# Gate and up products of one feed-forward block taken together, and a larger count for an exponential in the build-time planner

## The chip, the cores and the metric

The kernel runs on one core of a Trainium2 chip. The metric is the device time of one execution in microseconds (us); lower is better. The kernel before was timed three times: median 841.97 us, from 841.73 to 842.75.

## The reference

The input x (2048 rows of 512, bf16) goes through two branches, and a gate of one number per row mixes them:

```
g = sigmoid((x * gate_w).sum(-1, keepdims=True))
a = attention(x, wqkv) @ wo      # 32 heads of 16, no mask, softmax over 2048 keys
b = (silu(x @ w_gate) * (x @ w_up)) @ w_down     # 512 -> 1792 -> 512
return g * a + (1 - g) * b
```

Most of the work by far is the softmax: 32 heads x 2048 x 2048 exponentials. A head is only 16 wide, so the matmuls on either side of the exponential use a part of the array's rows or columns.

## The kernel before, in words

**Tiling.** Queries are cut into 4 blocks of 512 (QB), heads into 8 groups of 4 (G). One pair of these is a unit; there are 32. In a unit the keys are 16 tiles of 128 (KT). One key tile of one unit needs four score blocks, 128 keys by 512 queries, one for each head.

**Two ways to an exponential.** A score block goes one of two ways.
- ScalarE: two blocks at once into a two-bank PSUM tile (`s_t`, matmuls at most 64 rows high, two side by side), then one `Exp` over 128 x 1024 into `e_t` (`emit_pair`, L722). There are two such score tiles, so the score matmuls of pair k wait until the exponential of pair k-2 has read its tile.
- VectorE: one block into a single bank (`d_t`), one `tensor_scalar` from there into 16-bit integers (`y_t`), and after four of these, some passes over 128 x 2048 (`z_t`, `u_t`, two products) that correct the result. The last addition is made by a DMA that accumulates from GpSimd's queue (L802), or, for a tile near the end, by VectorE (`add_here`). `emit_d` (L755) holds this.

Either way the result is multiplied with the values in `o_ps` matmuls (four of 32 columns side by side, `pv`, L862), which collect in one bank per unit.

**The feed-forward branch and other side work.** It runs between the scores. For each query block there are 14 feed-forward blocks of 128 columns (FC). One has a gate product and an up product of four 128-row steps each. `two_banks` (L378) runs two accumulations at a time: each step is split into an upper and a lower half of 64 rows, and the halves of bank a and bank b run side by side. ScalarE takes tanh of the gate bank (`th`); VectorE makes `gs = (th + 1) * gate` from it and then `mt = 0.5 * gs * up`. `down_pieces` (L677) multiplies `mt` with w_down, 14 steps for two row tiles at once (`dps_a`, `dps_b`), and VectorE scales the result into `bblk`. `fin_pieces` and, for the last query block, `last_pieces` (L957, `a_l`) and `tail` (L963, `al`) apply wo and add.

Three single PSUM banks (`m_tile`, L335) serve all of this: gate and up, `dps`, `a_ps`, `a_l`, the q, k and v projections and every `d_t`. A two-bank piece starts only when two of them are free.

**What sets the order.** The Python code is a planner. At build time it keeps clocks for TensorE, VectorE and ScalarE (`plan.pe`, `plan.dve`, `plan.act`), adds a constant for each instruction it emits, and picks what comes next. Every instruction is then tied to its predecessor on its engine, so the order on the chip is the one that the planner wrote; the chip adds only waits. The numbers that matter here:
- `ACT_US` (L745): 0.906 counted for an exponential of 1024 columns. From it follow `s_end`, when a score tile is free, and `room`, how much time TensorE has before the next score pair; side work is put in as far as it fits.
- `v_unit` (L1290) gives a key tile to VectorE when its clock plus a lead is short of the time at which ScalarE would get there.
- A filler of four narrow matmuls (`o_ps<-xT`) is emitted where over 0.4 us of room are left and TensorE had little work just before.
- Side work is a list of chains with release and due slots (`Pacer`, L47). `pace.credit` grows with what is due. A chain waits for its predecessors.
- `later` queues a VectorE operation with its expected ready time and, optionally, a key; `fill_dve` avoids taking two with the same key one after the other, since `spend_v` adds 0.13 for that.

**Gate and up before.** `gu_chain(i)` (L630) puts the gate product of block i and the up product of block i-1 into one two-bank run. There are 57 chains for 56 blocks: the first has only a gate product and the last only an up product, each in one bank and at full height. At the end of a chain the product `gated` of block i-1, whose `gs` is there from the chain before, drains the up bank; tanh and then `gs` of block i drain the gate bank. `w_load` fetches up weights one block and gate weights two blocks ahead.

**The end.** When only one `o_ps` group is left, `tail(0)` completes all chains still open in the order of their due slots, and issues the first five of ten `al` matmuls. The last `o_ps` group follows, then the other five, the denominators of the last unit (`dt`, `rt`, `rps`), its scaled output, the last wo products, and four stores. This is the same in both kernels.

Of the kernel before, what the change touches and what calls it, by code (L numbers as in the profile page):

```python
# [9 lines left out]
ALU = mybir.AluOpType  # L10
AX = mybir.AxisListType
BF16 = mybir.dt.bfloat16
# [66 lines left out]
def kernel(  # L79
# [12 lines left out]
    nc = tc.nc  # L92
    P = 128
    x = A_x.flatten_outer_dims()
    S, D = x.shape
    F = B_w_gate.shape[1]
# [4 lines left out]
    DC = D // P  # L101
    FC = F // P
    KT = S // P
    QBW = 512
    QB = S // QBW
# [26 lines left out]
    work = ctx.enter_context(tc.tile_pool(name="work", bufs=2))  # L132
    etp = ctx.enter_context(tc.tile_pool(name="etp", bufs=EB))
    vex = ctx.enter_context(tc.tile_pool(name="vex", bufs=1))
    ffnw = ctx.enter_context(tc.tile_pool(name="ffnw", bufs=3))
# [20 lines left out]
    def mm(*args, **kw):  # L156
        return ordered(nc.tensor.matmul(*args, **kw))  # L157
# [10 lines left out]
    vec = Ordered()  # L168


    xT = big.tile([P, DC, S], BF16, name="xT")
# [4 lines left out]
    for c0 in (D, 0):  # L176

        nc.scalar.dma_start(out=wqk[:, :, c0:c0 + 64],
                            in_=A_wqkv[:, c0:c0 + 64].rearrange("(dc p) c -> p dc c", p=P))
# [29 lines left out]
    mt = big.tile([P, FC, QBW], BF16, name="mt")  # L209
# [39 lines left out]
    for h in range(8):  # L249
        c = 2 * (h % 4) + h // 4  # L250
# [32 lines left out]
    plan = Plan()  # L283
# [5 lines left out]
    def spend(mode, mms, ready=0.0):  # L289

        plan.seq += 1
        work_at.append((plan.pe, mms))
        plan.pe = max(plan.pe + (0.1 if mode != plan.mode else 0.0), ready) + (0.226 if mode == "F" else 0.216) * mms
        plan.mode = mode

    def later(cost, f, ready=None, key=None):

        c = plan.chain
        if c is not None:
            c.owed += 1  # L300
        ready = plan.pe + 0.25 if ready is None else ready
        owed.insert(sum(o[0] <= ready for o in owed), (ready, cost, f, c, key))
# [75 lines left out]
    def two_banks(n, name, a, b, end, stop=True):  # L378

        st = {}  # L380

        def pc(k):
            v, i = divmod(k, n)

            def f():
                if k == 0:
                    while m_ready(2) is None:
                        stuck()
                    st["a"], st["b"] = m_tile(name + "_a"), m_tile(name + "_b")
                if k == n:  # L390
                    sync(ordered(nc.tensor.nop()), st["half"])
                    spend("R", 0.1 if st["seq"] < plan.seq else 1.5)
                for ps, (w, r), h in ((st["a"], a(i), v), (st["b"], b(i), 1 - v)):
                    rows = slice(64 * h, 64 * h + 64)
                    st["half"] = mm(ps[:, :], lhsT=w[rows, :], rhs=r[rows, :], start=(k == i == 0),
                                    stop=(stop and k == 2 * n - 1), tile_position=(64 * h, 0), skip_group_check=True)
                spend("R", 1)
                st["seq"] = plan.seq
                if k == 2 * n - 1:
                    end(st["a"], st["b"])  # L400
            return f
        return [(1, pc(k), 2 if k == 0 else 0, "R", st if k == n else None) for k in range(2 * n)]
# [213 lines left out]
        later(0.5, end, plan.act + 0.2)  # L616


    FS = [(qb, fc) for qb in range(QB) for fc in range(FC)]
    w_gate, w_up, gs_of = {}, {}, {}  # L620

    def w_load(i, gate):
        if i < len(FS):
            w = ffnw.tile([P, DC, P], BF16, tag="wg" if gate else "wu", name="wg" if gate else "wu")
            fc = FS[i][1]
            nc.sync.dma_start(out=w[:], in_=(B_w_gate if gate else B_w_up)[:, fc * P:(fc + 1) * P].rearrange(
                "(dc p) f -> p dc f", p=P))
            (w_gate if gate else w_up)[i] = w

    def gu_chain(i):  # L630

        def rows(w_of, k):
            return lambda dc: (w_of[k][:, dc, :], xT[:, dc, FS[k][0] * QBW:(FS[k][0] + 1) * QBW])

        def gated(up):
            vec.scalar_tensor_tensor(out=mt[:, FS[i - 1][1], :], in0=gs_of.pop(i - 1)[:], scalar=0.5, in1=up[:, :],
                                     op0=ALU.mult, op1=ALU.mult)
            m_free(up, plan.dve)

        def gate(gp):  # L640
            th = work.tile([P, QBW], BF16, tag="th", name="th")
            flush_act(plan.pe + 0.4)
            act(out=th[:], in_=gp[:, :], func=ACT.Tanh, scale=0.5)
            plan.act = max(plan.act, plan.pe + 0.25) + 0.48

            def f():
                gs = work.tile([P, QBW], BF16, tag="gs", name="gs")
                vec.scalar_tensor_tensor(out=gs[:], in0=th[:], scalar=1.0, in1=gp[:, :], op0=ALU.add, op1=ALU.mult)
                m_free(gp, plan.dve)
                gs_of[i] = gs  # L650
            later(0.6, f, plan.act + 0.25)

        def both(gp, up):
            later(0.6, lambda: gated(up))
            gate(gp)

        if 0 < i < len(FS):
            return two_banks(DC, "gu", rows(w_gate, i), rows(w_up, i - 1), both)
        st = {}
        get, end = (rows(w_gate, 0), gate) if i == 0 else (rows(w_up, i - 1), lambda p: later(0.6, lambda: gated(p)))  # L660

        def pc(h):
            def f():
                if h == 0:
                    st["p"] = m_tile("gu")
                for dc in (2 * h, 2 * h + 1):
                    w, r = get(dc)
                    mm(st["p"][:, :], lhsT=w, rhs=r, start=(dc == 0), stop=(dc == DC - 1))
                spend("F", 2)
                if h == 1:  # L670
                    end(st["p"])
            return f
        return [(2, pc(0), True), (2, pc(1), False)]

    scaled = set()

# [65 lines left out]
        pairs[0] += 1  # L742

    exps = []
    ACT_US = 0.906  # L745

    def flush_act(before=None):

# [302 lines left out]
    for v in range(2):  # L1051
        vec.scalar_tensor_tensor(out=q0[0][:, v, :], in0=bp0[:, :], scalar=vsel[:, v:v + 1],
                                 in1=q0[0][:, v, :], op0=ALU.mult, op1=ALU.add)
# [3 lines left out]
                            op0=ALU.is_gt, op1=ALU.mult)  # L1057
    vec.scalar_tensor_tensor(out=bsel[:, :], in0=lo_t[:], scalar=0.5, in1=far_t[:],
                                   op0=ALU.is_lt, op1=ALU.mult)
# [47 lines left out]
    gates = [pace.add(gate_pieces(2 * i), 36 + 7 * i, 44 + 7 * i) for i in range(KT // 2)]  # L1107
    gates = [pace.add([(0.2, gate_end, False)], 40, 106, gates)]

    prev = []  # L1110
    fin_prev = []
    f0, f1 = 72, SLOTS - 8
    per = (f1 - f0) / QB
    for qb in range(QB):
        a0 = f0 + per * qb
        for i in range(FC * qb + (qb > 0), FC * qb + FC + 1):
            pcs = gu_chain(i)

            def first(f=pcs[0][1], i=i):
                if i == 0:  # L1120
                    w_load(0, True)
                    w_load(0, False)
                    w_load(1, True)
                w_load(i + 1, False)
                w_load(i + 2, True)
                f()
            pcs = [(pcs[0][0], first) + pcs[0][2:]] + pcs[1:]
            c = pace.add(pcs, 58, a0 + per * (0.6 if qb < QB - 1 else 0.68) * (i + 1 - FC * qb) / (FC + 1), prev)
            prev = [c]
        for tq in range(0, TQ, 2):  # L1130
            c = pace.add(down_pieces(qb, tq), 0 if qb else 100, a0 + per * (0.6 + 0.3 * (tq + 2) / TQ if qb < QB - 1 else 0.68 + 0.32 * (tq + 2) / TQ), prev + fin_prev + gates)
            prev = [c]
        last = qb == QB - 1
        fin_prev = []
        if last:
# [321 lines left out]
```

## Time and profile before

| what | before |
|---|---|
| median of 3 runs | 841.97 us |
| profiled execution, own time | 841.97 us |
| its span (first to last instruction) | 840.3 us |
| ScalarE busy | 815.2 us (97%) |
| VectorE busy | 785.5 us (93%) |
| TensorE matmuls busy | 759.7 us (90%) |
| mean granted TensorE clock | 0.998 |

The span is what the instructions of the program cover; 1.67 us of the execution's own time lie around it. A group in the profile is named by line, engine, operation and its tiles (output<-inputs); all matmuls have L157, all ScalarE instructions L160 and nearly all VectorE instructions L166, because helpers record them, so the tiles tell them apart. Busy time of TensorE is modelled for its end, and instructions overlap: an exponential of 1173 ns does not hold up the next for as long. Steps between starts are therefore taken from timelines.

### The profile page before, as it was taken

The page shows a single profiled execution, that of the slowest core. Times are in us where ns is not written, and L with a number is a line of the kernel's source. Part 1 is how long each engine was busy: PE and PEld are TensorE (multiplying, and loading weights), DVE is VectorE, ACT ScalarE, POOL GpSimd, SP SyncE. Part 2 cuts the span into 40 slices and gives each one's busy share as a digit, 9 for nine tenths or more (in the row PEclk, how much of TensorE's full clock was granted, in tenths as well). Part 3 has the DMA queues.
Part 4 walks back from the last instruction along what each step waited for, and adds up shares of the span by engine and source line. Part 5 has one row for each costly group of instructions (what it writes and reads, how often), then busy time and mean ns, then how long its engine had stood idle before and what let it go on. Part 6 is the DMA issues. An engine that isn't in the chain of part 4 may idle for free. (4 is left out here: it accounts for less than half of the span.)

```text
span 840.3 us, 16080 instructions
## 1 busy us (share of the span) xinstructions
PE 759.7 (90%) x5987; PEld 260.4 (31%) x6020; DVE 785.5 (93%) x1141; ACT 815.2 (97%) x916; POOL 94.9 (11%) x120
## 2 busy tenths in 40 slices
PE   7899899899989999999899998898999988998986
PEld 3222232233333333233333332222333322332322
DVE  6999998989999989999999899989999999999895
ACT  3999999999999999999999999999999999999996
POOL 5010100100101011110111101010011011000110
PEclk9999999999999999999999999999999999999999
DMA  9432252544455433554445435453544445363240
GB/s 204 128 70 45 57 98 58 108 92 86 96 104 111 92 80 73 108 114 92 99 88 107 80 87 105 92 107 74 104 90 80 91 95 108 89 124 60 58 95 26
DMA packets 101127, 77.18 MB, mean 92 GB/s; under 512 B 77728, under 2 KB 89592, under 8 KB 101048
## 3 DMA queue, kind: packets, MB, share of 16 engines
q0 software_dynamic: 12384, 45.09, 28.7%
q1 hardware_dynamic: 86792, 30.60, 15.5%
q8 instruction: 47, 0.77, 0.4%
q10 hardware_dynamic: 1872, 0.46, 0.2%
q14 instruction: 32, 0.26, 0.1%
HBM read 20.83 MB, written 2.34 MB: 28 GB/s over the span
## 5 line engine op out<-in xcount | busy, mean ns | idle before, releaser
L160 ACT ACTIVATE e_t<-s_t 128x1024 bf16<-128x1024 f32 x850 | 797.0, 1173 | 5.3 <-PE s_t L157 5.2
L157 PE MATMUL s_t<-qx,kaug 64*128 64x512 bf16 x1376 | 279.3, 380 | 51.0 <-ACT e_t L160 44.6
L157 PEld LDWEIGHTS <-kaug 64*128 64x128 bf16 x2048 | 140.3, 93 | 341.4 <-issue 306.5
L166 DVE TENSOR_SCALAR y_t<-d_t 128x512 uint16<-128x512 f32 x348 | 229.0, 682 | 17.9 <-PE d_t L157 15.1
L157 PE MATMUL o_ps<-e_t,vaug 128*32 128x512 bf16 x1700 | 160.0, 389 | 3.0 <-DVE osb L166 2.9
L157 PE MATMUL gu_b<-xT,wu 64*128 64x512 bf16 x440 | 133.1, 375 | 0.4 <-DVE y_t L166 0.2
L157 PE MATMUL gu_a<-xT,wg 64*128 64x512 bf16 x440 | 132.4, 375 | 0.0
L157 PE MATMUL d_t<-qx,kaug 64*128 64x512 bf16 x288 | 105.3, 377 | 4.6 <-DVE y_t L166 1.6
L157 PEld LDWEIGHTS <-vaug 128*32 128x32 bf16 (+1 forms) x2084 | 44.8, 94 | 139.0 <-issue 138.1
L802 POOL DMA_DIRECT2D y_t<-u_t x43 | 40.5, 943 | 356.2 <-PE s_t L157 165.6
L802 POOL DMA_DIRECT2D y_t<-kaug x36 | 36.6, 1016 | 294.8 <-PE s_t L157 141.3
L157 PE MATMUL dps_b<-wd_t,mt 64*128 64x512 bf16 x224 | 65.6, 375 | 0.0
L157 PE MATMUL dps_a<-wd_t,mt 64*128 64x512 bf16 x224 | 65.3, 375 | 0.0
L166 DVE TENSOR_SCALAR z_t<-y_t 128x2048 uint16<-128x2048 uint16 x87 | 60.1, 691 | 2.1
L166 DVE TENSOR_SCALAR y_t<-y_t 128x2048 uint16<-128x2048 uint16 x87 | 59.5, 684 | 1.4 <-DMA y_t<-kaug 1.4
L166 DVE TENSOR_TENSOR u_t<-u_t 128x2048 f16<-128x2048 f16 x43 | 52.6, 1223 | 1.1
L166 DVE TENSOR_TENSOR u_t<-u_t,z_t 128x2048 f16<-128x2048 f16 x43 | 52.3, 1216 | 0.0
L157 PE MATMUL s_t<-q,kaug 64*128 64x512 bf16 x216 | 43.8, 386 | 4.7 <-ACT e_t L160 4.0
L166 DVE TENSOR_TENSOR kaug<-kaug 128x2048 f16<-128x2048 f16 x37 | 45.2, 1222 | 0.9
L157 PEld LDWEIGHTS <-wg 64*128 64x128 bf16 (+1 forms) x444 | 41.2, 94 | 15.6 <-issue 1.8
L157 PEld LDWEIGHTS <-wu 64*128 64x128 bf16 (+1 forms) x444 | 41.3, 94 | 12.7 <-issue 0.9
L166 DVE TENSOR_TENSOR kaug<-kaug,z_t 128x2048 f16<-128x2048 f16 x37 | 45.0, 1215 | 0.0
(136 smaller groups left out, 631.0 us busy)
## 6 DMA issues: line engine op xcount, KB each, us to landing
y_t<-u_t POOLq DMA_DIRECT2D x43, 512.0 KB, 4.9
y_t<-kaug POOLq DMA_DIRECT2D x36, 512.0 KB, 4.9
wg<-in_B_w_gate_dram SPq DMA_DIRECT2D x56, 128.0 KB
wu<-in_B_w_up_dram SPq DMA_DIRECT2D x56, 128.0 KB
y_t<-wd_t POOLq DMA_DIRECT2D x7, 512.0 KB, 4.6
on<-osb SPq DMA_DIRECT2D x120, 16.0 KB
rb<-rr SPq DMA_DIRECT2D x15, 128.0 KB
wd_t<-in_B_w_down_dram SPq DMA_DIRECT2D x7, 256.0 KB
```

The source lines that it names most:

```text
L157: return ordered(nc.tensor.matmul(*args, **kw))
L160: ordered(nc.scalar.activation(*args, **kw))
L166: return lambda *a, **kw: ordered(f(*a, **kw))
L802: nc.gpsimd.dma_start(out=ya, in_=ua, accum_op=ALU.add)
```

## The change

Three edits:
1. `gu_chain(qb, fc)` now pairs the gate product and the up product of the same block. There are 56 chains, all of two banks. When one ends, tanh is emitted, and two VectorE operations, `gate` (makes `gs`, frees the gate bank) and `gated` (makes `mt`, frees the up bank), are queued with the same ready time, behind the tanh, and the same key.
2. Both weights of a block are loaded together, two blocks ahead. The due slots are spread over 14 chains a query block, not 15.
3. `ACT_US` is 0.92 in place of 0.906.

The loop in `tail` that completes open chains is not touched.

```diff
-    def gu_chain(i):
...
-        def gated(up):
-            vec.scalar_tensor_tensor(out=mt[:, FS[i - 1][1], :], in0=gs_of.pop(i - 1)[:], scalar=0.5, in1=up[:, :],
-                                     op0=ALU.mult, op1=ALU.mult)
-            m_free(up, plan.dve)
...
-        def both(gp, up):
-            later(0.6, lambda: gated(up))
-            gate(gp)
-
-        if 0 < i < len(FS):
-            return two_banks(DC, "gu", rows(w_gate, i), rows(w_up, i - 1), both)
...
+    def gu_chain(qb, fc):
+        st = {}
+
+        def load():
...
+        def done_gu(gp, up):
             th = work.tile([P, QBW], BF16, tag="th", name="th")
             flush_act(plan.pe + 0.4)
             act(out=th[:], in_=gp[:, :], func=ACT.Tanh, scale=0.5)
             plan.act = max(plan.act, plan.pe + 0.25) + 0.48
 
+            def gate():
+                st["gs"] = work.tile([P, QBW], BF16, tag="gs", name="gs")
+                vec.scalar_tensor_tensor(out=st["gs"][:], in0=th[:], scalar=1.0, in1=gp[:, :],
+                                         op0=ALU.add, op1=ALU.mult)
                 m_free(gp, plan.dve)
+
+            def gated():
+                vec.scalar_tensor_tensor(out=mt[:, fc, :], in0=st["gs"][:], scalar=0.5, in1=up[:, :],
+                                         op0=ALU.mult, op1=ALU.mult)
+                m_free(up, plan.dve)
+            later(0.6, gate, plan.act + 0.25, (qb, fc))
+            later(0.6, gated, plan.act + 0.25, (qb, fc))
+        return load, two_banks(DC, "gu", rows("g"), rows("u"), done_gu)
...
-    ACT_US = 0.906
+    ACT_US = 0.92
...
-                w_load(i + 1, False)
-                w_load(i + 2, True)
+                if ahead:
+                    gu[ahead][0]()
...
-            c = pace.add(pcs, 58, a0 + per * (0.6 if qb < QB - 1 else 0.68) * (i + 1 - FC * qb) / (FC + 1), prev)
+            c = pace.add(pcs, 58, a0 + per * (0.6 if qb < QB - 1 else 0.68) * (fc + 1) / FC, prev)
```

Since the planner works with clocks, these edits move instructions far from where they stand. Counted in the two built programs:

| instructions | before | changed |
|---|---|---|
| exponentials on ScalarE (`e_t`, 1024 columns) | 850 | 848 |
| key tiles on VectorE (`y_t`, four blocks each) | 87 | 88 |
| of these added by VectorE, not by DMA | 1 | 0 |
| filler groups of four narrow matmuls | 9 | 28 |
| half-height gate + up matmuls (full-height) | 440 + 440 (4 + 4) | 448 + 448 (0) |
| tanh; `gs`; `mt` | 56; 56; 56 | 56; 56; 56 |
| weight loads of gate + up | 56 + 56 | 56 + 56 |
| exponentials after the last tanh | 62 | 33 |

After the last score pair, TensorE's order in the changed program is: one `o_ps` group, six pairs of `dps`, one `o_ps` group from a VectorE tile, two pairs of `dps`, ten pairs of `a_l`, five `al`, the last `o_ps` group. In the kernel before it is: one `o_ps` group, one pair of `a_l`, five `al`, the last `o_ps` group. What follows is equal.

More of the change, by code (lines that the diff above doesn't have):

```diff
@@ L616, in gate_end, with rows @@
         later(0.5, end, plan.act + 0.2)
[L619 to L628, printed above, removed]
-    def gu_chain(i):
-        def rows(w_of, k):
-            return lambda dc: (w_of[k][:, dc, :], xT[:, dc, FS[k][0] * QBW:(FS[k][0] + 1) * QBW])
-        def gated(up):
-            vec.scalar_tensor_tensor(out=mt[:, FS[i - 1][1], :], in0=gs_of.pop(i - 1)[:], scalar=0.5, in1=up[:, :],
-                                     op0=ALU.mult, op1=ALU.mult)
-            m_free(up, plan.dve)
-        def gate(gp):
+    def gu_chain(qb, fc):
+        st = {}
+        def load():
+            st["wg"] = ffnw.tile([P, DC, P], BF16, tag="wg", name="wg")
+            nc.sync.dma_start(out=st["wg"][:], in_=B_w_gate[:, fc * P:(fc + 1) * P].rearrange("(dc p) f -> p dc f", p=P))
+            st["wu"] = ffnw.tile([P, DC, P], BF16, tag="wu", name="wu")
+            nc.sync.dma_start(out=st["wu"][:], in_=B_w_up[:, fc * P:(fc + 1) * P].rearrange("(dc p) f -> p dc f", p=P))
+        def rows(which):
+            return lambda dc: (st["w" + which][:, dc, :], xT[:, dc, qb * QBW:(qb + 1) * QBW])
+        def done_gu(gp, up):
             th = work.tile([P, QBW], BF16, tag="th", name="th")
@@ L644, in gate @@
             plan.act = max(plan.act, plan.pe + 0.25) + 0.48
-            def f():
-                gs = work.tile([P, QBW], BF16, tag="gs", name="gs")
-                vec.scalar_tensor_tensor(out=gs[:], in0=th[:], scalar=1.0, in1=gp[:, :], op0=ALU.add, op1=ALU.mult)
+            def gate():
+                st["gs"] = work.tile([P, QBW], BF16, tag="gs", name="gs")
+                vec.scalar_tensor_tensor(out=st["gs"][:], in0=th[:], scalar=1.0, in1=gp[:, :],
+                                         op0=ALU.add, op1=ALU.mult)
                 m_free(gp, plan.dve)
-                gs_of[i] = gs
-            later(0.6, f, plan.act + 0.25)
-        def both(gp, up):
-            later(0.6, lambda: gated(up))
-            gate(gp)
-        if 0 < i < len(FS):
-            return two_banks(DC, "gu", rows(w_gate, i), rows(w_up, i - 1), both)
[L659 to L673, printed above, removed]
+            def gated():
[5 more added lines that the diff above has]
+        return load, two_banks(DC, "gu", rows("g"), rows("u"), done_gu)
     scaled = set()
@@ L1108 @@
     gates = [pace.add([(0.2, gate_end, False)], 40, 106, gates)]
+    gu = {(qb, fc): gu_chain(qb, fc) for qb in range(QB) for fc in range(FC)}
+    order_ = [(qb, fc) for qb in range(QB) for fc in range(FC)]
     prev = []
@@ L1115, with first @@
         a0 = f0 + per * qb
-        for i in range(FC * qb + (qb > 0), FC * qb + FC + 1):
-            pcs = gu_chain(i)
-            def first(f=pcs[0][1], i=i):
-                if i == 0:
-                    w_load(0, True)
-                    w_load(0, False)
-                    w_load(1, True)
-                w_load(i + 1, False)
-                w_load(i + 2, True)
+        for fc in range(FC):
+            load, pcs = gu[(qb, fc)]
+            i = order_.index((qb, fc))
+            ahead = order_[i + 2] if i + 2 < len(order_) else None
+            def first(f=pcs[0][1], load=load, i=i, ahead=ahead):
+                if i == 0:
+                    load()
+                    gu[order_[1]][0]()
+                if ahead:
+                    gu[ahead][0]()
                 f()
             pcs = [(pcs[0][0], first) + pcs[0][2:]] + pcs[1:]
-            c = pace.add(pcs, 58, a0 + per * (0.6 if qb < QB - 1 else 0.68) * (i + 1 - FC * qb) / (FC + 1), prev)
+            c = pace.add(pcs, 58, a0 + per * (0.6 if qb < QB - 1 else 0.68) * (fc + 1) / FC, prev)
             prev = [c]
```

## Prediction

> **What bounds the kernel now.** I read the busy times first, then the costliest groups, the list of waits, and the timelines of ScalarE, TensorE and VectorE near the end.
>
> ```profile
> PE 759.7 (90%) x5987; PEld 260.4 (31%) x6020; DVE 785.5 (93%) x1141; ACT 815.2 (97%) x916; POOL 94.9 (11%) x120
> ...
> L160 ACT ACTIVATE e_t<-s_t 128x1024 bf16<-128x1024 f32 x850 | 797.0, 1173 | 5.3 <-PE s_t L157 5.2
> L157 PE MATMUL s_t<-qx,kaug 64*128 64x512 bf16 x1376 | 279.3, 380 | 51.0 <-ACT e_t L160 44.6
> L166 DVE TENSOR_SCALAR y_t<-d_t 128x512 uint16<-128x512 f32 x348 | 229.0, 682 | 17.9 <-PE d_t L157 15.1
> ```
>
> ScalarE is busy 97% of the span, nearly all of it in 850 exponentials, before which it idles 5.3 us in all. TensorE, before its score matmuls, stands 51.0 us, mostly for ScalarE to give a score buffer back. So the exponentials set the pace, with VectorE (93%) close behind. The wait list says the same from both sides:
>
> ```profile
> PE s_t L157 <- ACT e_t L160: 51.3, 159, 1.0
> ...
> ACT e_t L160 <- PE s_t L157: 5.2, 8, 1.5
> ```
>
> The timeline of ScalarE (start, length, count, idle before) shows where the stream begins and ends:
>
> ```profile
> 18.75 2.98 ACT L160 ACTIVATE e_t<-s_t 128x1024 bf16<-128x1024 f32 x3 [0.47 <-PE s_t L157]
> ...
> 773.69 0.78 ACT L160 ACTIVATE th<-gu_a 128x512 bf16<-128x512 f32 x1
> 774.16 37.88 ACT L160 ACTIVATE e_t<-s_t 128x1024 bf16<-128x1024 f32 x41
> 812.43 19.36 ACT L160 ACTIVATE e_t<-s_t 128x1024 bf16<-128x1024 f32 x21 [0.39 <-PE s_t L157]
> 835.63 0.69 ACT L160 ACTIVATE mt<-a_l_b,gval 128x512 bf16<-128x512 f32 x1 [3.84 <-PE a_l_b L157]
> ```
>
> The last 21 exponentials take 19.36 us, and one lasts 1.17 on average, so the step is (19.36 - 1.17) / 20 = 0.91 us. The last tanh, and with it the last gate product, comes 62 exponentials before the end. The stream ends at 831.8; from there to 840.3 is a tail on TensorE and VectorE.
>
> **Time of the profiled run.** It took 841.97 us, which is also the median of the three. Its span is 840.3, so 1.67 us lies around it; I add the same to the new span.
>
> **Step 1, the count of exponentials.** I counted both built programs. The changed one has 848 exponentials on ScalarE for 850 and 88 tiles (of four 512-column blocks) on VectorE for 87. Two fewer steps of 0.91 us are **-1.8 us**, if the stream stays as dense.
>
> Here a rule stands against the trace. ScalarE: Activation LUTs, section What ACT_TABLE_LOAD costs, gives an ACTIVATE with immediate operands as 186 ns + 0.833 ns per element, less 93 ns for overlap; at 1024 elements that is an estimate of 0.946 us. By it even 0.920 is too small, and two steps would be 1.9 us. The row says 0.91, so the planner's old 0.906 was close and 0.920 counts some 10 ns too many.
>
> **Step 2, the extra VectorE tile.** By VectorE's timeline it is four evictions of 0.60, two 16-bit passes of some 0.72, two products of 1.14 and a last pass of 0.60: 6.7 us. One in-place addition of 1.2 us goes, since the last tile is now added by DMA. Net **+5.5 us of VectorE work**. Cover: VectorE is idle 840.3 - 785.5 = 54.8 us, though some 20 of it lies in the prologue and the tail. Over stretches of 85 exponentials in the built order, the first left out, VectorE's instructions at the steps of its timeline come to at most 0.99 of ScalarE's in the changed program, and 1.01 in the old. So I take +0.5 us; ends 0 and +5.5.
>
> **Step 3, pairing gate with up of one block.** 448 + 448 half-height matmuls stand for 440 + 440 and 4 + 4 full-height ones, which is the same work within a step or two; the 56 + 56 VectorE products and the 56 tanh stay. The 56 + 56 weight loads stay on SP's queue; an up load is now issued two blocks ahead, with its gate load, not one, and TensorE's wait list names neither. What changes is how long the PSUM banks are held. In the old pairing the up bank is drained by one product whose other operand has long been there; in the new one it must outlast the tanh, the first product and the second: 0.6 us and more longer, 56 times, out of three shared banks. A two-bank chain starts only when two are free, so the feed-forward work falls behind its due times. The built order shows it: the last tanh has **33** exponentials behind it, not 62. Cost in the stream: nothing, hidden under the 51.3 us that TensorE waits for ScalarE; if that cover were gone, 56 holds of 0.6 us would be 34 us, which I exclude because the pieces between two scores, at the steps of TensorE's timeline, sum to 0.847 us a step on average in the new order and 0.843 in the old, and go beyond 0.91 in 152 places, 162 before.
>
> **Step 4, fillers.** The changed program has 28 filler groups of four narrow matmuls, not 9: the planner now sees more free room. One costs at most two changes of tile shape and its own pass, 0.32 + 0.33 us by the rows below, 19 x 0.65 = 12.4 us; they stand only where TensorE would wait. Zero taken. TensorEngine Tiling (Array Packing), section Key Properties, says a change of tiling mode drains TensorE. The rows agree that a change costs 0.1 us over the 0.21 step; by the rule alone the fillers speak against the change, and where a slot is full they would cost up to that 12.4.
>
> **Step 5, the tail.** This decides. TensorE's timeline, first with pairs in one shape, then from the last score on:
>
> ```profile
> 801.31 0.37 PE L157 MATMUL dps_b<-wd_t,mt 64*128 64x512 bf16 x1
> 801.33 0.38 PE L157 MATMUL dps_a<-wd_t,mt 64*128 64x512 bf16 x1
> 801.53 0.37 PE L157 MATMUL dps_b<-wd_t,mt 64*128 64x512 bf16 x1
> ...
> 830.01 0.39 PE L157 MATMUL s_t<-qx,kaug 64*128 64x512 bf16 x2 [0.52 <-ACT e_t L160]
> 830.33 0.40 PE L157 MATMUL o_ps<-e_t,vaug 128*32 128x512 bf16 x4
> 830.66 0.39 PE L157 MATMUL a_l_a<-bblk,ident 64*128 64x512 bf16 x1
> 830.67 0.39 PE L157 MATMUL a_l_b<-bblk,ident 64*128 64x512 bf16 x1
> 830.99 0.82 PE L157 MATMUL al<-wo_t,on 128*128 128x512 bf16 x2
> 831.64 0.38 PE L157 MATMUL al<-wo_l,osb 128*128 128x512 bf16 x1
> 831.86 0.38 PE L157 MATMUL al<-bblk,ident 128*128 128x512 bf16 x1
> 832.17 0.40 PE L157 MATMUL o_ps<-e_t,vaug 128*32 128x512 bf16 x4
> ```
>
> Before, after the last score at 830.01 only one a_l pair and five al matmuls stand ahead of the last o_ps, at 832.17: 2.16 us. In the changed order there stand, in this sequence: o_ps, six dps pairs, o_ps from a VectorE tile, two dps pairs, all ten a_l pairs, five al, the last o_ps. With 0.32 into the o_ps shape, 0.33 out of it, and 0.215 a pair: o_ps at 0.32, dps from 0.65, the y_t o_ps at 0.65 + 5 x 0.215 + 0.31 = 2.03, dps at 2.36 and 2.58, done at 2.96 (0.38 long). Now a wait: a_l needs two of three banks, dps held two, so the second must be evicted by VectorE first:
>
> ```profile
> 793.17 0.74 DVE L166 TENSOR_SCALAR bblk<-dps_a,ge 128x512 bf16<-128x512 f32 x1
> 793.83 0.74 DVE L166 TENSOR_SCALAR bblk<-dps_b,ge 128x512 bf16<-128x512 f32 x1
> ```
>
> 0.74 with 0.06 on either side (an estimate: the copy of the last o_ps starts at 832.62, 0.05 behind its end): a_l runs from 3.82. Nine steps of 0.215, and 0.3 where the second row half waits for the first (I bound it by 0 and 0.4, the length of a matmul): last pair at 6.06. al at 6.39, its fifth at 7.27, the last o_ps at 7.58. That is 7.58 - 2.16 = **+5.4 us**. Queued behind it on TensorE is the whole rest: last o_ps, its copy, denominators, final products and stores, 840.3 - 832.17 = 8.1 us as before.
>
> Also in this queue, o_ps from the last VectorE tile waits for its DMA addition. The last d_t is 13 scores ahead of the end (11.8 us); its chain is 0.9 to the end of eviction, 1.4 two passes, 1.3 two evictions, 2.3 two products, 0.5 + 4.9 issue and landing (the page's median), 0.7 last pass: 12.0, so ready near 0.2, needed at 2.03. Cover 1.8 us; a landing 3 us late would cost 1.2.
>
> **Sum.** 840.3 - 1.8 + 0.5 + 5.4 = 844.4; with 1.67, **846.1 us**, +0.5%.
>
> **Rivals.**
> A, VectorE becomes the bound: planned against 0.920 and run against 0.91, its work lags ScalarE by 10 ns x 848 = 8 us unless its idle time absorbs it. For: 93% busy, 348 evictions, PSUM banks that only it frees. Against: the stretch sums of step 2. Price: all 5.5 and up to half of the 8 come through, 851 to 855, taken 852.
>
> B, faster: from 18.75 to the start of the last exponential (831.79 - 1.17) are 811.9 us, 56 tanh steps of 0.47 take 26, so the mean step is 786 / 849 = 0.925, not 0.91: 13 us are lost in short hold-ups. A planner that leaves 0.920 may spread TensorE's pieces better. Deciding point: it must win back more than 5.8 us (846.1 to 840.3), 45% of that 13. At half, 6.5 us, 839.6. Against: the longest ScalarE idle is 1.5 us and eight cases are 5.2 us in all.
>
> C, the tail costs less: DMA, eviction and bank hand-over hide better, or a few hold-ups go, by 3 to 5 us: 842.5, within 0.2%.
>
> D, the change does not do what it says: the forced completion ahead of the last tiles is in both programs, so it has no price of its own.
>
> **How the numbers follow.** About 0.2% (840.3 to 843.7) is what a measurement can tell from no change. Forecast, 843.7 to 850: 0.62. A: 0.12. C: 0.16. B: 0.10. Faster 0.10, same 0.16, slower 0.74. The range 842.5 to 851.5 takes in the tail less 2 and VectorE's 5.5 in full; about 0.2 stays out, most of B with the low half of C, and the high half of A.
>
> **What would show it.** Right: 848 e_t; the last one starting near 829; eight dps and ten a_l pairs after the last score; the last o_ps some 7.5 us behind that score. Wrong: ScalarE idle before e_t grown from 5.3 to over 10 us with VectorE as the releaser (A); a mean step clearly under 0.925 (B); the y_t o_ps held by a late DMA addition.

## The result and the profile after

The changed kernel took a median of 847.31 us over four executions (845.84 to 848.29), the kernel before 842.36 over four: ratio 1.0053, interval 1.0028 to 1.0078. The forecast was 846.1 us, a ratio of 1.005. Measured a second time (`e5_changed_again`, below) it took 848.67 against 842.20: 1.0077, 1.0061 to 1.0094.

The profiled execution took 848.13 us with a span of 846.2. Its page, busy times and the costliest groups of ScalarE and of the score matmuls (busy, mean ns, idle before):

```profile
PE 768.2 (91%) x6075; PEld 267.6 (32%) x6104; DVE 788.0 (93%) x1149; ACT 814.6 (96%) x914; POOL 90.5 (11%) x122
...
L160 ACT ACTIVATE e_t<-s_t 128x1024 bf16<-128x1024 f32 x848 | 795.1, 1156 | 6.4 <-PE s_t L157 5.3
L157 PE MATMUL s_t<-qx,kaug 64*128 64x512 bf16 x1380 | 283.3, 383 | 49.0 <-ACT e_t L160 43.0
```

The engines are as busy as before, ScalarE still waits for little (6.4 us), and TensorE still stands 49.0 us before its score matmuls, 43.0 of them for ScalarE. Nothing has changed sides. The timeline of ScalarE at the end shows the last tanh, the exponentials after it, and the new wait:

```profile
800.74 0.83 ACT L160 ACTIVATE th<-gu_a 128x512 bf16<-128x512 f32 x1
801.22 11.35 ACT L160 ACTIVATE e_t<-s_t 128x1024 bf16<-128x1024 f32 x12
813.00 19.36 ACT L160 ACTIVATE e_t<-s_t 128x1024 bf16<-128x1024 f32 x21 [0.43 <-PE s_t L157]
841.55 0.69 ACT L160 ACTIVATE mt<-a_l_b,gval 128x512 bf16<-128x512 f32 x1 [9.20 <-PE a_l_b L157]
```

The wait for the last a_l has grown from 3.84 to 9.20 us. TensorE's timeline from the last score says why:

```profile
830.57 0.39 PE L157 MATMUL s_t<-qx,kaug 64*128 64x512 bf16 x2
830.89 0.40 PE L157 MATMUL o_ps<-e_t,vaug 128*32 128x512 bf16 x4
831.23 0.39 PE L157 MATMUL dps_a<-wd_t,mt 64*128 64x512 bf16 x1
...
832.63 0.40 PE L157 MATMUL o_ps<-y_t,vaug 128*32 128x512 bf16 x4
...
833.18 0.38 PE L157 MATMUL dps_a<-wd_t,mt 64*128 64x512 bf16 x1
833.19 0.38 PE L157 MATMUL dps_b<-wd_t,mt 64*128 64x512 bf16 x1
833.40 0.38 PE L157 MATMUL a_l_a<-wo_t,on 64*128 64x512 bf16 x1
834.40 0.37 PE L157 MATMUL a_l_b<-wo_t,on 64*128 64x512 bf16 x1 [0.62 <-DVE bblk L166]
...
836.60 0.38 PE L157 MATMUL a_l_b<-bblk,ident 64*128 64x512 bf16 x1
836.90 0.82 PE L157 MATMUL al<-wo_t,on 128*128 128x512 bf16 x2
...
838.09 0.40 PE L157 MATMUL o_ps<-e_t,vaug 128*32 128x512 bf16 x4
```

From the last score to the last o_ps are 838.09 - 830.57 = 7.52 us, 5.36 more than the 2.16 before. The wait of a_l_b for the eviction of the first dps bank stands where it was put. VectorE's side of it, with the last pass of the DMA-added tile ahead:

```profile
830.52 0.69 DVE L166 TENSOR_SCALAR y_t<-y_t 128x2048 uint16<-128x2048 uint16 x1 [4.93 <-DMA y_t<-u_t]
833.60 0.75 DVE L166 TENSOR_SCALAR bblk<-dps_a,ge 128x512 bf16<-128x512 f32 x1 [2.38 <-PE dps_b L157]
```

**What the sum did not have.** In this profile the stream of exponentials ends no earlier: the last one starts at 831.11 here, and started at 830.59 before, though there are two fewer. So of the 5.9 us between the spans 5.4 are the tail and 0.5 the stream. The table by stretches, around one such place, shows where the stream lost its gain (TensorE's granted clock is the figure behind the counts):

```profile
366.00:370.00 4.00, 3.66 (x32) 1.42 (x33) 3.90 (x6) 4.00 (x6) 1.17 (x1) 1.00 0.39 76
370.00:374.00 4.00, 3.27 (x20) 0.83 (x20) 4.00 (x7) 3.73 (x5) 0.86 (x1) 0.73 1.04 181
374.00:378.00 4.00, 4.00 (x35) 1.24 (x33) 3.93 (x7) 3.49 (x4) 0.00 (x0) 0.84 0.37 71
```

Read in steps of 2 us, the clock falls to 0.5 and comes back after 3.4 us: 1.70 us of full clock are lost, the same at each drop of these two profiles. Within it a matmul takes 0.63 us and not 0.38, the scores are late, and ScalarE idles. The profile before has one such drop while exponentials run (130 to 134 us), this one three (24, 372 and 734 us). From 5 us ahead of each drop to 4 us behind it ScalarE loses 2.6 us before and 6.4 us after. The Trainium skill, TensorE: Matmul & The Clock Gate, section Part 1: The HAM clock gate, says that the clock is set to half or full by how busy TensorE was in a free-running window of 3413 ns. The rows agree in the length and the factor. In the 3.4 us ahead of the drop at 372, TensorE began seven passes of 0.215 us, at most 1.5 us of work.

Not all that is lost there is the work of the clock. Of the 2.6 us before, 1.5 go ahead of the drop, to one late score; of the 6.4 us after, 1.8 go ahead of the drop at 24 us, and the kernel before loses the same there without a drop. A hold-up that leaves TensorE short of work costs time by itself, and the slow clock behind it costs more. How much more can be read at 24 us, where TensorE's order is still the same in both kernels, but the clock fell (23.70 to 27.11) in the changed kernel alone. ScalarE's rows, first before, then changed:

```profile
23.25 7.54 ACT L160 ACTIVATE e_t<-s_t 128x1024 bf16<-128x1024 f32 x8 [1.53 <-PE s_t L157]
```

```profile
23.21 1.02 ACT L160 ACTIVATE e_t<-s_t 128x1024 bf16<-128x1024 f32 x1 [1.53 <-PE s_t L157]
24.60 1.02 ACT L160 ACTIVATE e_t<-s_t 128x1024 bf16<-128x1024 f32 x1 [0.36 <-PE s_t L157]
26.00 1.02 ACT L160 ACTIVATE e_t<-s_t 128x1024 bf16<-128x1024 f32 x1 [0.37 <-PE s_t L157]
27.39 2.86 ACT L160 ACTIVATE e_t<-s_t 128x1024 bf16<-128x1024 f32 x3 [0.37 <-PE d_t L157]
```

From the first of these exponentials to the fourth are 4.18 us with the drop and 2.85 without: 1.3 us for one drop.

The mean granted clock of an execution counts these drops: 1.70 us of 842 are 0.002. The spans follow it. The 26 executions of the kernel before on the chip of the first four experiments run from 839.3 to 841.4 us where the clock was 0.996 to 0.998, and are 844.5 and 846.6 at 0.988. A straight line through span against clock, over all 74 executions of the kernel before beside the experiments, falls by 1.0 us for each 0.002. So a drop, with the hold-up that can go ahead of it, costs about 1 us, and kernels are best compared at equal clock as well as by their medians. At equal clock the ten executions of the changed kernel lie 2.4 to 4.8 us above that line, 3.3 on the mean; the tail and the two exponentials of the prediction (-1.8 + 5.4) come to 3.6. The rest of the measured loss, 1.4 us in the first comparison and 2.9 in the second, I put down to the lower clock and the hold-ups that come with it; no run changed the clock alone.

### The profile page after: what moved, and what is told of

Read it like the earlier page. It is cut to its first block, busy times and chain, and to the rows that moved or that the text cites. A ratio compares the mean times of both kernels' runs of the same rounds, so it can differ in the third digit from the quotient of the medians.

```text
span 846.2 us, 16282 instructions
## 1 busy us (share of the span) xinstructions
PE 768.2 (91%) x6075; PEld 267.6 (32%) x6104; DVE 788.0 (93%) x1149; ACT 814.6 (96%) x914; POOL 90.5 (11%) x122
## 3 DMA queue, kind: packets, MB, share of 16 engines
q1 hardware_dynamic: 86792, 30.60, 15.4%
## 4 chain that ended last, share of the span: by engine, by line
DVE 26%; ACT 19%; PE 18%; issue 5%; DMA 3%; DVEq 0%; ACTq 0%
ACT e_t L160 18%; DVE y_t L166 9%; PE s_t L157 6%; DVE kaug L166 5%; DVE u_t L166 5%; PE o_ps L157 3%; PE dps_a L157 3%; DVE z_t L166 2%; PE d_t L157 2%; DVE mt L166 2%; DVE gs L166 2%; PE dps_b L157 2%; ACT th L160 1%; PE gu_a L157 1%; DVE osb L166 1%
## 5 line engine op out<-in xcount | busy, mean ns | idle before, releaser
L157 PE MATMUL s_t<-qx,kaug 64*128 64x512 bf16 x1380 | 283.3, 383 | 49.0 <-ACT e_t L160 43.0
L166 DVE TENSOR_SCALAR y_t<-d_t 128x512 uint16<-128x512 f32 x352 | 231.4, 682 | 12.4 <-PE d_t L157 11.1
L157 PE MATMUL gu_b<-xT,wu 64*128 64x512 bf16 x448 | 135.4, 377 | 0.5 <-DVE y_t L166 0.4
L157 PE MATMUL gu_a<-xT,wg 64*128 64x512 bf16 x448 | 134.9, 377 | 0.0
L778 POOL DMA_DIRECT2D y_t<-kaug x37 | 33.6, 907 | 313.2 <-PE s_t L157 136.2
L157 PEld LDWEIGHTS <-wg 64*128 64x128 bf16 x448 | 41.9, 94 | 18.6 <-issue 4.9
L157 PEld LDWEIGHTS <-wu 64*128 64x128 bf16 x448 | 42.0, 94 | 13.8 <-issue 0.2
```

The source lines that it names most:

```text
L166: return lambda *a, **kw: ordered(f(*a, **kw))
L778: nc.gpsimd.dma_start(out=ya, in_=ua, accum_op=ALU.add)
```

## The experiments

Theory 1: the new pairing makes the feed-forward work late, and its rest runs after the last score. Theory 2, rival: the count of 0.920 and the load on VectorE cost in the stream. Theory 3, formed on the trace after: sparse stretches of TensorE halve its clock. Times are medians with the ratio to the kernel before on the same chip and its interval; "tail" is from the start of the last score to the start of the last o_ps, in the profiled run.

### The count alone

```diff
 # kernel before
-    ACT_US = 0.906
+    ACT_US = 0.92
```

> The kernel before with the count of 0.920 alone; the pairing stays the old one. Built: 850 exponentials, 87 VectorE tiles, 21 filler groups, last tanh 75 exponentials before the end, and after the last score the same TensorE work as before (one o_ps, one a_l pair, five al, the last o_ps). Theory 1 (the pairing makes the feed-forward work late and its rest runs after the last score): no tail, so 842 us, within 1.5 us of the kernel before. Theory 2 (the larger count itself costs, because VectorE and TensorE are planned against a slower ScalarE): 845 to 848, most of the change's loss.

Measured: 844.21 us, 1.0013 (0.9998 to 1.0027); tail 2.16; median clock 0.996. That is 1.2 us above the kernel before, with an interval that takes in none, as theory 1 has it. The count does not make the tail, and by the interval it costs at most 2.3 us. That it is free is not shown: at equal clock all twelve executions lie 0.9 to 2.1 us above the line through the kernel before.

### The pairing alone

```diff
 # changed kernel
-    ACT_US = 0.92
+    ACT_US = 0.906
```

> The changed kernel with 0.906 counted for an exponential, so the new pairing alone. Built: 850 exponentials, 87 VectorE tiles; the feed-forward work is so late that after the last score there stand eight gate and up pairs, 56 dps pairs, ten a_l pairs and five al ahead of the last o_ps. Theory 1: gate and up until 2.96 us after the last score starts, the up bank free after tanh and one product at 4.45, 28 dps pairs until 10.5, an eviction, 28 more until 17.6, an eviction, a_l and al until 22.2, last o_ps at 22.6 where it was 2.16: 842 + 20.4 = 862 us, 858 to 866. Theory 2: with the old count back the time is 842 to 844.

Measured: 865.85 us, 1.0267 (1.0235 to 1.0300); tail 22.84, reckoned 22.6. The two edits pull in opposite directions: the larger count leaves room between scores in which the late work still finds a place. With the old count and the new pairing, the whole gate and up product of the last feed-forward block (eight pairs) and all down products of the last query block (56 pairs) are left for the end.

### The last block's chains due earlier

```diff
 # changed kernel
-            c = pace.add(pcs, 58, a0 + per * (0.6 if qb < QB - 1 else 0.68) * (fc + 1) / FC, prev)
+            c = pace.add(pcs, 58, a0 + per * (0.6 if qb < QB - 1 else 0.50) * (fc + 1) / FC, prev)
```

> The changed kernel, with one number different: in the last query block the gate and up chains are due at 0.50 of the block's slots, not 0.68. Pairing and the count of 0.920 stay. Built: 850 exponentials, 87 VectorE tiles, 22 filler groups; the last dps pair is five scores ahead of the end, and after the last score stand one o_ps, three a_l pairs, five al, the last o_ps. Theory 1: the tail is 2.16 + 2 x 0.215 = 2.6 us, so 842.4, within 1.5 us. Theory 2: the count is still 0.920 and the pairing the new one, so the loss stays: 845 to 848.

Measured: 845.24 us, 1.0027 (1.0010 to 1.0044); tail 2.59. Half a hit. The tail is what was expected to the hundredth, 0.4 us above the kernel before, but the time lies in theory 2's range and not in theory 1's: 2.2 us of loss stay, with a median clock of 0.9905. Its two executions at 0.995 have spans of 841.2 and 841.8, the three of the kernel before at 0.995 have 840.9 to 841.3. What stays goes with the clock; why this order loses more of it is not shown.

### No key on the two products

```diff
 # changed kernel
-            later(0.6, gate, plan.act + 0.25, (qb, fc))
-            later(0.6, gated, plan.act + 0.25, (qb, fc))
+            later(0.6, gate, plan.act + 0.25)
+            later(0.6, gated, plan.act + 0.25)
```

> The changed kernel without the key on its two VectorE operations, so that the planner may put the product that drains the up bank right behind the one that drains the gate bank. Built: 850 exponentials, 87 VectorE tiles, 21 filler groups, last tanh 61 exponentials before the end; after the last score one o_ps, one a_l pair, a second o_ps, five al, the last o_ps. Theory 1, with the hold of the up bank as the cause of the lateness: tail 2.16 + 0.65 = 2.8 us, and some back-to-back dependent products on VectorE (up to 56 x 0.13 = 7 us of VectorE time, hidden): 842.6, within 1.5 us. Theory 2: 845 to 848, as the count is 0.920; and if the dependent products come through, more.

Measured: 848.77 us, 1.0064 (1.0043 to 1.0085); tail 3.34. A miss. The work is in time and the tail 1.2 us above the kernel before (0.47 of it because the second o_ps waits for the last exponential), yet the loss is as large. From the start of `gs` to the next instruction VectorE now takes 0.76 us on the mean, in the changed kernel 0.61: 56 x 0.15 = 8.5 us of which the planner knows nothing, as it no longer has the key to add for. At a clock of 1.000 the span is still 844.5. I read this as VectorE time that is no longer hidden, which the last experiment tests by itself.

### The tail thinned

```diff
 # changed kernel, two_banks
                 for ps, (w, r), h in ((st["a"], a(i), v), (st["b"], b(i), 1 - v)):
+                    if pairs[0] == 848 and 0 < i < n - 1:
+                        continue
```

> The changed kernel once more, unaltered, so that the next three stand beside it on one chip. Theory 1 (rest of the feed-forward work after the last score, 7.5 us from that score to the last o_ps in place of 2.2): 4 us above the kernel before, 846 to 848 if that stays at 843. Theory 3 (the granted clock of TensorE halves for 3.4 us now and then, and each time costs about 1 us) says how the single runs spread: the span falls by about 1 us for each 0.002 of mean granted clock.

> The changed kernel with part of the tail left out: after the last score pair, the accumulations of dps and a_l issue only their first and last step of each half, so seven dps pairs and six a_l pairs are not computed. Everything ahead of the last score is the changed order, instruction for instruction. Theory 1: the last o_ps starts 4.6 us after the last score, not 7.5 (o_ps 0.32, y_t o_ps once its last pass is done at 0.7, one dps pair until 1.4, eviction and hand-over until 2.3, four a_l pairs, five al): 2.9 us below the changed kernel. Rival (the tail's matmuls lie beside other work, say the DMA addition or the evictions): less than 1 us below.

Measured: the changed kernel 848.67 us, tail 7.51, median clock 0.990; thinned 842.64, 1.0019 (1.0005 to 1.0033), tail 4.63, clock 0.995. The medians lie 6.0 apart, which is more than the tail; the clocks differ too. At the clock that both have, 0.995, the spans are 843.7 and 840.6 to 841.6 (840.8 in the middle): 2.9 us, the expected number.

The profiled run of the changed kernel (845.62 us, the fastest of the six) also shows the stream: the last exponential starts at 828.70, 1.9 us earlier than before, and the tail is the same 7.5 us. -1.9 + 5.4 = 3.5 is what separates the spans (843.7 and 840.3). Its rows on TensorE:

```profile
828.17 0.39 PE L157 MATMUL s_t<-qx,kaug 64*128 64x512 bf16 x2
...
835.68 0.40 PE L157 MATMUL o_ps<-e_t,vaug 128*32 128x512 bf16 x4
```

TensorE's timeline of the thinned kernel, which leaves 13 pairs out:

```profile
829.21 0.39 PE L157 MATMUL s_t<-qx,kaug 64*128 64x512 bf16 x2
...
830.48 0.38 PE L157 MATMUL a_l_a<-wo_t,on 64*128 64x512 bf16 x1
831.47 0.37 PE L157 MATMUL a_l_b<-wo_t,on 64*128 64x512 bf16 x1 [0.62 <-DVE bblk L166]
...
833.84 0.40 PE L157 MATMUL o_ps<-e_t,vaug 128*32 128x512 bf16 x4
```

The wait for the eviction is the same 0.62 us; only the pairs have gone. 13 pairs at 0.215 us are 2.8 us: a pair after the last score costs its full step.

### More fillers in the kernel before

```diff
 # kernel before, the bound below which a filler is put in
-                    w for t, w in work_at[-24:] if t > plan.pe - 3.0) < 6.5:
+                    w for t, w in work_at[-24:] if t > plan.pe - 3.0) < 10.0:
```

> The kernel before, with one number different: a filler is put in where TensorE had less than 10.0 units of work in the last 3 us, not 6.5. Built: 850 exponentials, 87 VectorE tiles, 120 filler groups for 9, after the last score one more o_ps (0.66 us of tail). Theory 3: TensorE is no more sparse anywhere, the mean granted clock goes to 0.999 or over from 0.995, and 2 to 3 us come back: 841, 1 to 2.5 us below the kernel before with the tail's 0.66 counted. Rival (fillers take the place of score matmuls, as each costs up to 0.65 us with its changes of shape): 845 or more.

Measured: 851.14 us, 1.0109 (1.0096 to 1.0122). A miss for theory 3, and not by the rival's mechanism. One group of TensorE's timeline, and the table by stretches:

```profile
82.13 0.62 PE L157 MATMUL o_ps<-y_t,vaug 128*32 128x512 bf16 x4 [5.19 <-DVE y_t L166]
```

```profile
76.00:80.00 4.00, 0.75 (x8) 0.34 (x7) 3.93 (x6) 2.33 (x3) 0.85 (x1) 1.00 0.62 122
80.00:84.00 4.00, 1.08 (x8) 0.22 (x7) 2.73 (x4) 0.00 (x0) 0.85 (x1) 0.64 0.22 42
84.00:88.00 4.00, 4.00 (x24) 0.70 (x20) 1.35 (x2) 2.11 (x3) 0.00 (x0) 0.50 0.52 103
88.00:92.00 4.00, 4.00 (x20) 0.62 (x16) 2.04 (x5) 2.71 (x3) 0.00 (x0) 0.58 0.00 0
```

The shifted order put one o_ps of a VectorE tile ahead of the tile's last pass. It waits 5.2 us at the head of TensorE's queue, every score stands behind it, and TensorE stays so empty that the clock is halved for 10.2 us behind it. One wrong place in a planned order costs 9 us.

### More fillers in the changed kernel

The same edit in the changed kernel.

> The changed kernel with the same bound of 10.0 units for a filler. Built: 850 exponentials, 87 VectorE tiles, 153 filler groups for 28, and, as the order shifts, the last dps pair eight scores ahead of the end and only two o_ps and five al after the last score (2.1 us of tail). Theories 1 and 3 together: no tail and a clock of 0.999, so 840.5 to 842, though pairing and count are the changed ones. Theory 2 (the count of 0.920 and the extra hold of the banks cost in the stream itself): 844 to 847.

Measured: 840.35 us, 0.9976 (0.9965 to 0.9988); tail 2.65; median clock 0.997, with two of seven executions at 1.000. Faster than both kernels. So the new pairing shows no cost in the stream once little is left over and the clock stays up.

### No fillers in the changed kernel

The same place with `< 0.0`.

> The changed kernel without any filler group (0 for 28). Built: 848 exponentials and 88 VectorE tiles as in the changed kernel, last tanh 33 exponentials before the end, and three dps pairs fewer after the last score (0.6 us). Theory 3 (sparse stretches of TensorE are what halves its granted clock): more of them are left, so the mean clock falls below the changed kernel's 0.990 to 0.994 and the time does not fall by more than the tail's 0.6 us: 847 to 850. Rival (a filler costs its 0.65 us, because it stands between score pairs): 28 x 0.65 = 18 us would come back at most, and anything below 845 speaks for it.

Measured: 850.40 us, 1.0074 (1.0051 to 1.0096); tail 6.43; median clock 0.9855 (the changed kernel had 0.990). The tail is 1.1 us shorter, 0.4 of it because a_l_b waits 0.19 us for the eviction and not 0.62, and 28 fillers are gone, and yet the ratio is that of the changed kernel. At 0.995 its span is 843.9, the changed kernel's 843.7. A filler costs nothing that can be seen, and without them the clock is lower, as theory 3 says; whether that difference in clock is more than chance, six executions each do not tell.

### The count and more fillers, with the old pairing

```diff
 # kernel before
-    ACT_US = 0.906
+    ACT_US = 0.92
...
-                    w for t, w in work_at[-24:] if t > plan.pe - 3.0) < 6.5:
+                    w for t, w in work_at[-24:] if t > plan.pe - 3.0) < 10.0:
```

> The kernel before with both numbers: 0.920 counted for an exponential and 10.0 units as the bound for a filler; the pairing is the old one. Built: 848 exponentials, 88 VectorE tiles, 137 filler groups, 74 exponentials after the last tanh, nothing of the feed-forward work after the last score but one a_l pair. Theories 1 and 3: two exponentials fewer are 1.8 us, tail as before, clock 0.998 or more: 839.5 to 841 where the kernel before has 842.5. Theory 2 (VectorE's tile more comes through): 844 or more. A single long hold-up as in the kernel before with that bound for fillers, which was 7 us long, can spoil it: then 848.

Measured: 837.72 us, 0.9931 (0.9917 to 0.9945); tail 2.16; every execution at a clock of 0.999 or 1.000. The best of all. Its page and its waits of ScalarE:

```profile
PE 790.1 (94%) x6532; PEld 266.3 (32%) x6532; DVE 784.7 (94%) x1149; ACT 814.1 (97%) x914; POOL 94.0 (11%) x122
```

```profile
ACT e_t L160 <- PE s_t L157: 2.0, 2, 1.5
```

ScalarE waits 2.0 us for scores in the whole run, 1.5 of it at the start. With 88 VectorE tiles, as in the changed kernel, the stream loses 15.4 us to steps above 0.904 us; the kernel before lost 17.5, 2.6 of them at its clock drop. Without those 2.6 that is 0.5 us more here; but 1.5 of the 2.6 are the late score ahead of the drop, which this order does not have. What the extra tile costs by itself is therefore not shown, only that it is not much.

### The same with a bound of 12.0

> As the one before, with 12.0 units as the bound for a filler. Built: 846 exponentials, 89 VectorE tiles, 236 filler groups. Theories 1 and 3: four exponentials fewer, 3.6 us, tail 0.3 us shorter, clock 0.999: 838 to 839. Theory 2: two VectorE tiles more are 13 us of work on an engine that is 93% busy, and part of it comes through: 842 or more.

Measured: 840.27 us, 0.9962 (0.9949 to 0.9975). A miss: two exponentials fewer did not pay. TensorE is 96% busy and waits only 11.8 us for score tiles, and in the profiled run ScalarE lost 2.7 us in one step at 799 us, just ahead of a drop of the clock. The trace shows that hold-up:

```profile
798.68 0.69 DVE L166 TENSOR_SCALAR kaug<-z_t 128x2048 f16<-128x2048 uint16 x1 [2.10 <-DMA y_t<-kaug]
801.29 0.58 PE L157 MATMUL d_t<-qx,kaug 64*128 64x512 bf16 x1 [2.41 <-DVE y_t L166]
```

VectorE waits for an adding DMA, its next eviction is late, and a d_t and the score behind it wait for that bank. It explains 2.7 us of this one run; whether the further VectorE tile or the 236 fillers brought the order about, and what the other executions lost, was not separated.

### VectorE work of which the planner does not know

```diff
 # kernel before, behind the product that makes gs
+                for _ in range(2):
+                    vec.memset(scratch[:], 0.0)
```

> The kernel before with two small VectorE memsets added after each of the 56 gate products, of which the planner knows nothing, so the order of all else is the old one. They take an estimated 0.07 to 0.1 us each (a memset of 64 words lasts 0.11 us in the trace, one of one word 0.06), 8 to 11 us of VectorE time in all, about as much as the changed kernel without keys spent on dependent products. Theory 1 (VectorE's 55 us of idle time hide such additions, as the 5.5 us of the extra tile were taken to be): at most 1 us above the kernel before. Theory 2 (VectorE is the second bound, and what it is given comes through): 4 to 9 us above it. A third or a half, 3 to 5 us, would say that the cover holds in some stretches only.

Measured: 847.17 us, 1.0052 (1.0033 to 1.0070); tail 2.16; median clock 0.996, beside it 0.995. The rows:

```profile
L166 DVE MEMSET scratch<- x112: 98/98/98, 162.9 to 780.9; 128x48 f32 x112
```

By VectorE's starts the memsets take 11.7 us of the queue, and `gs` ahead of them 0.04 us more each, 2 us. 4.4 us come through, a third. The number lies in theory 2's range as well as in the one for a partial cover, since the two overlap; that a third comes through and not all speaks for the cover in some stretches only. That work which the planner counts is laid beside other work, and work that it does not know about is paid for where VectorE is full, fits this and was not traced from place to place.

## Why the prediction was right, and where it was not

**The bound and the sign.** Right: ScalarE's stream sets the pace, and what stands behind the last score is added in full. At equal clock the sum was 0.8 us too high (4.1 for 3.3), and it had no term for the lower clock; the two errors are of opposite sign, so that the first median lies nearer to the forecast than the sum deserves.

**Step 5, the tail.** Right in mechanism and size: 7.52 us for the 7.58 worked out, from the order of the built program and the steps of the trace before. The wait for the eviction, the tile by DMA addition (its last pass over at 831.21, o_ps at 832.63, so 1.4 us of cover for the 1.8 given) and the half-row wait were all there. Shown by the thinned tail (2.9 us for 13 pairs) and the earlier due slots (tail 2.59).

**Step 1, two exponentials fewer.** Right in one of two profiles. In the second comparison's the last exponential starts 1.9 us earlier than before (828.70), near the 829 that the prediction named as its sign; in the first profile, with three drops of the clock, it starts 0.5 us later. Two exponentials fewer were not measured alone.

**Step 2, the extra tile at +0.5.** No run shows this term by itself. The kernel with the count and more fillers has the same 88 tiles and is the fastest of all, which leaves little room for the full 5.5 us. The reason given, that VectorE's idle time covers it, was too broad: unplanned VectorE work comes through by a third. To that extent rival A had a point, though its sign, ScalarE idle for over 10 us with VectorE as the releaser, did not show (6.4 us, for score matmuls).

**Step 3, the pairing.** The feed-forward work came late, as forecast; the size of the hold was wrong, and its part in the lateness is open. The text put the longer hold of the up bank at "0.6 us and more". By the two traces, from the end of a block's last gu_b matmul to the end of its mt product are 1.05 us in the median before and 4.05 after: 3.0 us, five times as much, because the bank waits for the tanh, `gs` and a product in between. That the bank hold is what makes the chains late was argued from this and from the order without the key, where the last tanh moves from 33 to 61 exponentials before the end. The trace of that order weakens the argument: there the hold is still 3.63 us, and the work is in time. With more fillers it is 3.73. No run changed the hold alone, so whether the hold is what makes the chains late stays open. That the new pairing makes them late, and not the count, is shown by the two runs with one of the two edits: the last tanh is 75 exponentials before the end with the count alone, and behind the last score with the pairing alone.

**Step 4, fillers at nothing.** Right for their price. What the step missed is what they are for: it read the mean clock of 0.998 as a constant and had no term for it. The measured losses, 5.0 and 6.5 us, exceed the forecast 4.1 (846.1 - 842.0) by 0.8 and 2.3, with median clocks of 0.995 and 0.990 (that of the kernel before was 0.996 in the second). No run shows a price of a filler by itself; the order with 137 of them is the fastest.

**Rival B** asked for 13 us of lost steps to be won back. They can be, in part: the kernel with old pairing, count and fillers is 5.4 us faster than the kernel before. The count alone did not do it (1.0013), and the fillers alone met the misplaced o_ps, so it takes both, or the fillers in an order without that wait.

**Open:** why the changed order has more drops of the clock than the old one. The held banks leave fewer pieces to put between scores, which would fit; it was not tried apart. A part is chance: the thinned kernel has the changed order at 24 us too, and its profile has no drop there.

## What to carry to other kernels

Where one engine's stream sets the time, read the built order behind its last instruction first: every piece left there costs its whole step, and it can be added up from the trace before to a tenth of a microsecond (7.52 for 7.58, 2.59 for 2.6, 4.63 for 4.6), or to half a microsecond where a wait appears that the sum did not have (3.34 for 2.8, 2.65 for 2.1). A cost can show up far from the edit, here as work that arrives late at the end. When a kernel's executions spread by a few microseconds, set each span beside its mean granted clock before explaining a difference, and look for the stretches of 3 to 4 us in which TensorE has little to do: both the hold-up and the slow clock behind it cost.

## What the runs showed of the hardware that was not expected

- A sparse TensorE can lose half its clock in mid-kernel: for 3.4 us (1.70 us of full clock), in some profiles for 6.8 (the count alone, at 207 us) and once for 10.2. On this kernel 3.4 us cost about 1 us.
- In each of the 14 profiles the clock changes only at whole multiples of 3.413 us from its first rise. While exponentials ran there were 33 drops; ahead of 32 of them the stretch of that length held at most eight passes of TensorE, ahead of one ten. It is not enough to be sparse: the kernel before has a stretch of six passes at 17.5 us and no drop behind it. What decides was not found.
- With 137 fillers of four narrow matmuls the clock did not drop while exponentials ran in the profiled run, and all six executions lie between 837.46 and 838.29 us; the kernel before on that chip spread from 841.77 to 845.50.
- Exponentials of 128 x 1024 follow each other at 0.904 us at best; 510 of the 792 steps from one to the next in the trace before take 0.904 or 0.905, and 163 more take 0.915 to 0.921.
- A change of tile shape on TensorE costs 0.10 us going into the four-column shape and 0.11 to 0.16 us coming out, over a step of 0.215.
